# Turning k in 32x32 blocks on VectorE, and subtracting its low part on GpSimd, from the fifth pair of heads on

## The chip, the cores and the metric

One core of a Trainium2 chip. The metric is the device time of one execution in microseconds (us). The kernel before takes 958.05 us, the median of three runs (957.85 to 958.69).

## The reference

Three stages, all in fp32:

```
# decay attention: q, k, v are (4, 8, 576, 64), f is (4, 8, 576)
scores = q @ k.T / sqrt(64);  cum = cumsum(log(clip(f)))
scores = where(causal, -1e9, scores + cum[i] - cum[j])
attn   = softmax(scores);  x = attn @ v          # x then is (2304, 512)
# MLP 1:  h = max(x @ w_in, 0);  x = (h * h) @ w_out             (d_ff 2048)
# MLP 2:  x = (sigmoid(x @ w_gate) * (x @ w_val)) @ w_out2       (d_ff 1536)
```

The change is in the attention. 4 x 8 heads are 16 pairs of heads (p = 0 to 15).

## The kernel before, in words

fp32 products are computed as three products of reduced-precision parts: an operand x is split into a high part (a copy in the rounded type fp32r) and a low part (x minus the high part), and high-low, low-high and high-high are added up in PSUM. So each of q and k needs a high part (`qh`, `kh`) and a low part (`ql`, `kl`), both laid out with the 64 features of two heads on the 128 partitions and the 576 tokens along the free dimension.

**Loads.** `load(p, which)` (L275) brings q, k or v of a pair into `nat[...]`, tokens on partitions: two DMAs with runs of 256 bytes (L282) and one for the last 64 tokens (L286). q and k have two buffers, `nat["k"][p % 2]`. All DMAs are issued by SyncE (SP), which takes them in the order in which they are written and waits at each until its buffer is free.

**Turning.** `TQ` and `TK` turn q and k with five TensorE transposes each (L376, 128x128, with an identity matrix) into a PSUM tile; four PSUM tiles of [128, 1024] go round as a ring (`ps2`), each use waiting for the last reader of the one four uses earlier. Then ScalarE writes `qh` (L440) and `kh` (L467), and VectorE `ql` (L444) and `kl` (L471), all out of PSUM.

**The rest of a pair.** `S2`, `S3`, `S01` and `S4` (L416, L510) are score products of the query blocks; `R` (L390) on VectorE adds the causal mask and takes the row minimum (scores are negated); `X` (L398) is the exponential with row sums on ScalarE; `N0`, `N2`, `N3` (L519 a TENSOR_SCALAR, L520 a reciprocal) invert the row sums on VectorE; `M` (L528) multiplies the rows by them on GpSimd; `G1` to `G4` (L539, L545) are TensorE transposes of the result, in which G3 reads what M3a and M3b wrote and G4 what M4 wrote; `E1` to `E4` evacuate them (odd ones ScalarE L424, even ones VectorE L426); `PV` (L573) multiplies with v; `xhi` (L590, ScalarE) and `xlo` (L588, VectorE) split the output into parts. `EL` and `EH` (L452) copy the last 64 rows of ql and qh on GpSimd for S4.

**The order.** The order of all engines is written out by hand: the string `ORDER` lists the steps of one iteration, each with a lag (`TK-1` in iteration `it` works on pair it + 1, `PV+2` on pair it - 2), and each engine gets its instructions in that order. An iteration's PV is TensorE's first large piece in the listing below; PV of pair p belongs to iteration p + 2. `ahead` hangs pieces of weight preparation in front of a step: VectorE's four conversion operations of a weight block (L149, L150, L153, L156) stand one each ahead of `xlo` in iterations 5 to 8 and again 9 to 12, and GpSimd's subtractions (L630) ahead of `M0a` in iterations 10, 11, 14 and 15.

In the old order, ScalarE has X2a, xhi, qh, kh, X0a one after the other; VectorE has R0b, N3, xlo, ql, kl, R4; GpSimd has M0a, M1a, M1b, M2a, M2b, M0b, M3b, M3a, M4, EL, EH.

Of the kernel before, what the change touches and what calls it, by code (L numbers as in the profile page):

```python
# [9 lines left out]
F32 = mybir.dt.float32  # L10
# [3 lines left out]
AF = mybir.ActivationFunctionType  # L14
ALU = mybir.AluOpType
# [26 lines left out]
def kernel(  # L42
# [13 lines left out]
    nc = tc.nc  # L56
    B, H, S, D = q.shape
    NT, DM = out.shape
    BH = B * H
    NP = BH // 2  # L60
# [186 lines left out]
    def tiles(n, name, shape, dt=F32):  # L247
        return [ap_.tile(shape, dt, name=f"{name}{i}") for i in range(n)]

    nat = {nm_: tiles(3 if nm_ == "v" else 2, nm_ + "n", [128, NC, 2, D]) for nm_ in "qkv"}  # L250
    qk = [{nm_: ap_.tile([128, S], F32R, name=f"{nm_}{i}") for nm_ in ("qh", "ql", "kh", "kl", "cr")} for i in range(2)]
# [15 lines left out]
    cum_b = pts[0:BH, 6 * S:6 * S + 3 * HALF].bitcast(BF16)  # L267

    ring = [0]

    def ps2():
        ring[0] += 1
        return pair_t[(ring[0] - 1) % 4]

    def load(p, which):  # L275
        b, h0 = divmod(2 * p, H)
        for src, nm_ in ((q, "q"), (k, "k"), (v, "v")):
            if nm_ not in which:
                continue
            t = nat[nm_][p % len(nat[nm_])]  # L280
            for i in range(2):
                nc.sync.dma_start(  # L282
                    out=t[:, 0:NF, i, :],
                    in_=src[b, h0 + i, 0:NF * 128, :].rearrange("(c p) d -> p c d", p=128),
                )
            nc.sync.dma_start(  # L286
                out=t[0:REM, NF, :, :],
                in_=src[b, h0:h0 + 2, NF * 128:S, :].rearrange("h p d -> p h d"),
            )
# [28 lines left out]
    def setup():  # L318
# [8 lines left out]
        for nm_ in "qk":  # L327
            for t in nat[nm_]:
                nc.gpsimd.memset(t[64:128, NF, :, :], 0.0)
        load(0, "qk")  # L330
        nc.vector.tensor_reduce(out=nm_t[0][:, 0:1], in_=ident[:, 0:111:22], axis=mybir.AxisListType.X, op=ALU.add)
        nc.vector.tensor_scalar(one_l, one_l.bitcast(F32), nm_t[0][:, 0:1], None, op0=ALU.mult)
# [10 lines left out]
        for nm_ in ("eh", "el"):  # L343
            nc.gpsimd.memset(qk[0][nm_].bitcast(F32), 0.0)
        cum_v = cum_s.bitcast(F32).rearrange("p (t s) -> p t s", t=3)
        load(1, "q")
        cr_load(0, cum_v)
        load(1, "k")
        cr_load(1, cum_v)
        nc.gpsimd.memset(maskc, 0.0)  # L350
# [23 lines left out]
    def transpose_in(t, x):  # L374
        for c in range(NC):
            nc.tensor.transpose(x[:, 128 * c:128 * c + 128], t[:, c, :, :].rearrange("p h d -> p (h d)"), ident)  # L376
        return x[:, 0:S]
# [24 lines left out]
    live = {}  # L402
# [25 lines left out]

    def TQ(p):
        x = ps2()  # L430
        live["kt", p] = ps2()
        if p > 2:
            live["s4", p - 1] = ps2()
            s4_decay(p - 1)
        live["q", p] = transpose_in(nat["q"][p % 2], x)
        if p + 2 < NP and p != 1:
            load(p + 2, "q")
# [20 lines left out]
        ends(p, "el", "ql")  # L458

    def TK(p):  # L460
        live["k", p] = transpose_in(nat["k"][p % 2], live.pop(("kt", p)))
        if p + 2 < NP and p != 1:
            load(p + 2, "k")

    def kh(p):
        d = qk[p % 2]
        nc.scalar.activation(out=d["kh"], in_=live["k", p], func=AF.Copy)  # L467

    def kl(p):
        d = qk[p % 2]  # L470
        nc.vector.tensor_tensor(out=d["kl"], in0=live.pop(("k", p)), in1=d["kh"].bitcast(F32), op=ALU.subtract)  # L471

    def S01(p):
        s = live.pop(("s01", p))
# [20 lines left out]
    def s4_decay(p):  # L495
        s = live["s4", p]
        for g in range(2):
            a, b = decay(p, slice(0, 128), slice(64, 192), slice(g * HALF, (g + 1) * HALF))
            nc.tensor.matmul(s[:, 512 * g:512 * g + HALF], lhsT=a, rhs=b, start=True, stop=False)
# [81 lines left out]
    def x_part(p, low):  # L581
# [8 lines left out]
                nc.scalar.activation(out=x[:, 0, xs], in_=i, func=AF.Copy)  # L590

    STEP = {
        "CR": CR, "TQ": TQ, "qh": qh, "ql": ql, "EH": EH, "EL": EL, "TK": TK, "kh": kh, "kl": kl,
        "S01": S01, "S2": S2, "S3": S3, "S4": S4, "PV": PV,
        "xhi": lambda p: x_part(p, 0), "xlo": lambda p: x_part(p, 1),
        "N0": lambda p: N(p, 0, 4), "N2": lambda p: N(p, 4, 6),
# [6 lines left out]
    for g in range(1, 5):  # L603
        STEP[f"G{g}"] = lambda p, g=g: G(p, g)
        STEP[f"E{g}"] = lambda p, g=g: E(p, g)
    ORDER = """
        CR-1 R3a+1 X3a+1 S01+0 R2a+0 M0a+1 R2b+0 X2a+0 M1a+1 PV+2 N3f+1 xhi+2 M1b+1 R1b+0 R1a+0
        R0a+0 R0b+0 N3+1 TQ-1 TK-1 M2a+1 qh-1 kh-1 M2b+1 S4+0 M0b+1 xlo+2 X0a+0 ql-1 G1+1 X1a+0 kl-1
        X0b+0 M3b+1 M3a+1 E1+1 G2+1 G3+1 M4+1 X1b+0 R4+0 E3+1 G4+1 E2+1 N0+0 S3+0 X2b+0 EL-1 X4+0
        E4+1 S2-1 R3b+0 N2+0 X3b+0 EH-1  # L610
    """.split()
# [23 lines left out]
    for m in range(2):  # L635
        b = 4 + 4 * m
# [22 lines left out]
    for it in range(min(lags), NP + max(lags)):  # L659
# [6 lines left out]
        for nm_, lag in steps:  # L666
            p = it - lag
# [129 lines left out]
    late = []  # L797
# [438 lines left out]
    for n, (z, key, m) in enumerate(items):  # L1236
# [12 lines left out]
        elif m % 2:  # L1249
            at(*slot(z + 6), *[part_fn(w_sum, key, m // 2, x) for x in range(4)])  # L1250
            for x in range(4):
                p = 42 * (m // 2) + x - 1
# [244 lines left out]
    for i, (j, u) in enumerate(dsteps):  # L1497
# [43 lines left out]
        for c in range(2 if i == 0 else 0, 3):  # L1541
            o = down(i, c)
            if u == NU2 - 1:
                e = rs[c]
# [61 lines left out]
```

## Time and profile before

| | |
|---|---|
| median of three runs | 958.05 us |
| the profiled execution | 958.46 us, of which its span is 956.7 us |
| TensorE matmul busy | 949.4 us (99%) |
| VectorE / ScalarE / GpSimd busy | 734.9 / 560.8 / 329.1 us |
| attention stage | the first 180 us or so |
| granted TensorE clock | 1.0 of full speed |

All times in the listings are us from the start of the span; a row of a timeline is start, length, engine, line, operation, output <- input, shapes and count, and in brackets the idle time of the engine before it with the engine whose work ended that idle time. A row can hold several instructions of one line (x3).

### The profile page before, as it was taken

The numbers are of one execution on the slowest core, as the hardware profiler recorded it, in microseconds if no ns is written. First come the engines' busy times: TensorE is split into PE (matmuls) and PEld (weight loads), VectorE is DVE, ScalarE is ACT, GpSimd is POOL, SyncE is SP. The second block draws the span as 40 slices with busy tenths as digits, with TensorE's granted clock in tenths as the row PEclk, the third lists the DMA queues.
The fourth block names the chain that finished last, engine by engine and source line by source line (L and its number), as shares of the span: only waits on it lengthen the run. The fifth ranks groups of instructions, "written<-read, shape, count | busy, mean of one in ns | idle before, by whom it ended". The sixth has DMA issues, their size and how long they took to land.

```text
span 956.7 us, 18030 instructions
## 1 busy us (share of the span) xinstructions
PE 949.4 (99%) x6315; PEld 912.9 (95%) x6315; DVE 734.9 (77%) x1458; ACT 560.8 (59%) x1148; POOL 329.1 (34%) x427
## 2 busy tenths in 40 slices
PE   8999999999999999999999999999999999999998
PEld 7888888999999999999999999999999999889998
DVE  7889888376666676688879989767676777698895
ACT  7888888476565665566556556544445455354432
POOL 8777878112111120047023255634243341300000
PEclk9999999999999999999999999999999999999999
DMA  5633330287888889667776612334333345764441
GB/s 124 167 88 90 90 85 17 64 260 253 275 271 276 272 276 314 216 202 208 229 220 196 190 56 95 124 105 144 116 116 127 125 168 198 256 220 143 149 133 67
DMA packets 159618, 160.88 MB, mean 168 GB/s; under 512 B 66312, under 2 KB 136284, under 8 KB 159528
## 3 DMA queue, kind: packets, MB, share of 16 engines
q1 hardware_dynamic: 159528, 159.74, 54.2%
q8 instruction: 49, 0.80, 0.4%
q14 instruction: 41, 0.34, 0.1%
HBM read 102.93 MB, written 56.73 MB: 167 GB/s over the span
## 4 chain that ended last, share of the span: by engine, by line
PE 75%; DMA 10%; DVE 7%; ACT 4%; issue 2%; POOL 1%; SPq 0%; ACTq 0%; DVEq 0%
PE ps L1100 27%; PE ps L1046 13%; PE ps L1446 9%; PE ps L1322 5%; PE pa L573 5%; PE pa L416 4%; PE pa L539 4%; DMA g<-gt 3%; PE ps L220 3%; DMA gl<-g 2%; DVE gt L206 2%; DVE gg L742 2%; PE pa L376 1%; DMA wraw<-in_moe_w_in_dram 1%; DMA wraw<-in_moe_w_out_dram 1%
## 5 line engine op out<-in xcount | busy, mean ns | idle before, releaser
L220 PE MATMUL ps<-xT,hl 128*128 128x384 f32 x1104 | 191.5, 334 | 0.0
L220 PEld LDWEIGHTS ps<-xT,hl 128*128 128x128 f32 x1104 | 191.4, 188 | 0.0
L1046 PE MATMUL ps<-gg,ao 128*128 128x384 f32 x1008 | 175.8, 335 | 0.7 <-DVE gg L742 0.6
L1046 PEld LDWEIGHTS ps<-gg,ao 128*128 128x128 f32 x1008 | 174.5, 188 | 1.8 <-DVE gg L742 1.5
L528 POOL TENSOR_TENSOR pt<-pt,sm 128x128 f32<-128x128 f32 (+2 forms) x142 | 105.4, 769 | 33.2 <-DVE sm L520 27.2
L1100 PE MATMUL ps<-xT,r 128*128 128x384 f32 x576 | 107.5, 334 | 0.0
L742 DVE TENSOR_TENSOR gg<-gl,gg 128x768 fp32r<-128x768 f32 x78 | 81.9, 1055 | 28.4 <-ACT gg L741 28.1
L741 ACT ACTIVATE gg<-gl 128x768 fp32r<-128x768 f32 x78 | 66.0, 846 | 64.0 <-DMA gl<-g 30.1
L1100 PEld LDWEIGHTS ps<-xT,r 128*128 128x128 f32 x576 | 100.6, 188 | 0.1
L206 DVE TENSOR_TENSOR gt<-gt 128x384 f32<-128x384 f32 x96 | 53.6, 599 | 57.3 <-ACT gt L229 55.8
L398 ACT ACTIVATE pt<-pt,nm 128x384 f32<-128x384 f32 (+2 forms) x144 | 82.9, 582 | 3.7 <-DVE nm L390 3.2
L390 DVE CUSTOM_DVE_ANT_0 pt<-pa,maskc 128x384 f32<-128x384 f32 (+2 forms) x144 | 66.9, 514 | 3.5 <-PE pa L416 3.2
L132 ACT ACTIVATE wtmp<-wraw 128x512 f32<-128x512 f32 x66 | 43.9, 665 | 33.5 <-DMA wraw<-in_moe_w_in_dram 16.9
L177 POOL TENSOR_TENSOR hl<-wf,hl 128x512 fp32r<-128x512 f32 x14 | 18.1, 1295 | 129.2 <-ACT hl L173 129.2
L804 POOL TENSOR_TENSOR xT<-yt,xT 128x384 fp32r<-128x384 f32 x12 | 17.7, 1482 | 118.0 <-ACT xT L800 118.0
L1100 PE MATMUL ps<-xT,f 128*128 128x384 f32 x288 | 55.7, 334 | 0.0
L1100 PE MATMUL ps<-t,r 128*128 128x384 f32 x288 | 54.1, 334 | 0.0
L229 ACT ACTIVATE gt<-gt 128x384 f32<-128x384 f32 x96 | 50.5, 526 | 3.1
L1100 PEld LDWEIGHTS ps<-xT,f 128*128 128x128 f32 x288 | 50.4, 188 | 0.0
L1100 PEld LDWEIGHTS ps<-t,r 128*128 128x128 f32 x288 | 50.3, 188 | 0.1
L228 ACT ACTIVATE gt<-ps 128x384 f32<-128x384 f32 x92 | 43.9, 477 | 8.4 <-PE ps L220 7.0
L1424 ACT ACTIVATE xT<-x 128x896 fp32r<-128x896 f32 x27 | 25.7, 954 | 36.8 <-DVE x L1416 16.4
(257 smaller groups left out, 1959.1 us busy)
## 6 DMA issues: line engine op xcount, KB each, us to landing
gl<-g SPq DMA_DIRECT2D x90, 384.0 KB, 3.7
g<-gt SPq DMA_DIRECT2D x168, 192.0 KB, 4.8
wraw<-in_moe_w_out_dram SPq DMA_DIRECT2D x28, 512.0 KB, 4.7
x<-g SPq DMA_DIRECT2D x72, 128.0 KB, 2.7
wraw<-in_moe_w_in_dram SPq DMA_DIRECT2D x16, 512.0 KB, 4.5
wraw<-in_moe_w_val_dram SPq DMA_DIRECT2D x12, 512.0 KB, 4.4
g<-pb SPq DMA_DIRECT2D x29, 192.0 KB, 1.9
wraw<-in_moe_w_gate_dram SPq DMA_DIRECT2D x10, 512.0 KB, 4.0
```

What stands on the lines that cost most here:

```text
L206: nc.vector.tensor_tensor(out=t, in0=a, in1=b_, op=ALU.subtract)
L220: nc.tensor.matmul(h, lhsT=a, rhs=xT[c][:, b_, t0:t0 + BT], start=(c == 0 and i == 0), stop=(c == KD - 1 and i == 2))
L229: nc.scalar.activation(out=r, in_=r, func=AF.Square)
L390: nc.vector.tensor_tensor_reduce(out=o, in0=s, in1=mask, scale=1.0, scalar=3.0e38, op0=ALU.add, op1=ALU.min, accum_out=nm_t[p % 2][:, c:c ...
L398: nc.scalar.activation(out=x, in_=x, func=AF.Exp, bias=nm_t[p % 2][:, c:c + 1], scale=-1.0, accum_out=sm_t[p % 2][:, c:c + 1])
L528: nc.gpsimd.tensor_tensor(out=x, in0=x, in1=sm_t[p % 2][:, c:c + 1].to_broadcast([128, e - a]), op=ALU.mult)
L573: nc.tensor.matmul(o[64 * h:64 * h + 64, 512 * half + s - lo:512 * half + hi - lo], lhsT=vn[:, c, h, :], rhs=pts[:, h * PW + c * PS + s:h ...
L741: nc.scalar.activation(out=s[:, 0], in_=t, func=AF.Copy)
L742: nc.vector.tensor_tensor(out=s[:, 1], in0=t, in1=s.bitcast(F32)[:, 0], op=ALU.subtract)
L1046: nc.tensor.matmul(o, lhsT=ws[:, a, u, cs], rhs=s[:, b_, u, :], start=(k_ in (0, 2, 5) and w == u == x == 0), stop=(w == NW - 1 and u == 1 ...
L1100: nc.tensor.matmul(o, lhsT=w[p][:, a, ws], rhs=operand(n, jj, b_, c), start=(first and c == x == 0), stop=(c == 1 and x == 2), skip_group_ ...
L1446: nc.tensor.matmul(o, lhsT=YR[i % 4][:, a, FROM[n]], rhs=b_op(n, u, b_), start=(x == u == y == 0), stop=(u == NU2 - 1 and y == 2), skip_gr ...
```

## The change

From pair TP = 4 on k is not loaded with tokens on partitions but in four DMAs, one for each quarter of 32 partitions: partition 32r + i holds, for the 18 blocks of 32 tokens, the 32 features of quarter r of token 32b + i, in runs of 128 bytes. One VectorE instruction (`TKv`) then turns each 32x32 block in place, so that the features of two heads stand on the partitions, in SBUF. `TK` does nothing for these pairs and the PSUM tile that it used is not taken from the ring. `kh` (new step `khe`) reads SBUF on ScalarE, placed after X2a and ahead of xhi; `kl` (new step `kle`) is a GpSimd subtraction, placed after M0b and ahead of M3b; the load of the pair after next follows it. Pairs 0 to 3 are as before.

```diff
+    TP = 4
+
+    def k_flat(p):
+        return nat["k"][p % 2].rearrange("p c h d -> p (c h d)")[:, 0:S]
...
             t = nat[nm_][p % len(nat[nm_])]
+            if nm_ == "k" and p >= TP:
+                for r in range(4):
+                    h, e = divmod(r, 2)
+                    nc.sync.dma_start(
+                        out=k_flat(p)[32 * r:32 * r + 32, :].rearrange("p (b j) -> p b j", j=32),
+                        in_=src[b, h0 + h, :, 32 * e:32 * e + 32].rearrange("(b i) j -> i b j", i=32),
+                    )
+                continue
...
     def TQ(p):
         x = ps2()
-        live["kt", p] = ps2()
+        if p < TP:
+            live["kt", p] = ps2()
...
     def TK(p):
+        if p >= TP:
+            return
...
+    def TKv(p):
+        if p >= TP:
+            nc.vector.transpose(out=k_flat(p), in_=k_flat(p))
+            live["k", p] = k_flat(p)
+
+    def kh(p, late):
+        if late == (p < TP):
+            nc.scalar.activation(out=qk[p % 2]["kh"], in_=live["k", p], func=AF.Copy)
+
+    def kl(p, late):
+        if late == (p < TP):
+            d, eng = qk[p % 2], nc.vector if late else nc.gpsimd
+            eng.tensor_tensor(out=d["kl"], in0=live.pop(("k", p)), in1=d["kh"].bitcast(F32), op=ALU.subtract)
+            if not late and p + 2 < NP:
+                load(p + 2, "k")
...
-        CR-1 R3a+1 X3a+1 S01+0 R2a+0 M0a+1 R2b+0 X2a+0 M1a+1 PV+2 N3f+1 xhi+2 M1b+1 R1b+0 R1a+0
-        R0a+0 R0b+0 N3+1 TQ-1 TK-1 M2a+1 qh-1 kh-1 M2b+1 S4+0 M0b+1 xlo+2 X0a+0 ql-1 G1+1 X1a+0 kl-1
+        CR-1 R3a+1 X3a+1 S01+0 R2a+0 M0a+1 R2b+0 X2a+0 M1a+1 PV+2 khe-1 N3f+1 xhi+2 M1b+1 R1b+0 R1a+0
+        R0a+0 R0b+0 N3+1 TKv-2 TQ-1 TK-1 M2a+1 qh-1 kh-1 M2b+1 S4+0 M0b+1 kle-1 xlo+2 X0a+0 ql-1 G1+1 X1a+0 kl-1
```

## Rows read from the trace of the kernel before

**Rows 1.** Busy time by stretch (stretch: length, then each engine, clock, DMA).
```profile
core 0: us, PE busy (x) PEld busy (x) DVE busy (x) ACT busy (x) POOL busy (x), PEclk, DMA share, GB/s
60.00:70.00 10.00, 10.00 (x103) 8.55 (x102) 8.98 (x31) 8.67 (x25) 7.25 (x13) 1.00 0.41 92
```

**Rows 2.** Chain of waits: start, length, what; the attention stage.
```profile
66.51 2.85 PE pa L573 x28
...
69.72 1.09 PE pa L376 x10
...
76.80 2.85 PE pa L573 x28
```

**Rows 3.** Timeline of PE's weight loads, G4 of two iterations.
```profile
83.81 0.58 PEld L545 LDWEIGHTS pa<-ident,pt 128*128 128x128 f32 x5
...
165.62 0.53 PEld L545 LDWEIGHTS pa<-ident,pt 128*128 128x128 f32 x5 [0.25 <-POOL pt L528]
```

**Rows 4.** Timeline of ACT: xhi, and the first instruction behind X2a.
```profile
79.70 0.71 ACT L590 ACTIVATE xT<-pa 128x256 fp32r<-128x256 f32 x2 [1.27 <-PE pa L573]
...
88.61 0.67 ACT L132 ACTIVATE wtmp<-wraw 128x512 f32<-128x512 f32 x1
```

**Rows 5.** Timeline of DVE: conversions, N3's first op, xlo, ql, kl.
```profile
58.67 0.40 DVE L149 TENSOR_SCALAR wtmp<-wtmp 128x512 f32<-128x512 f32 x1
...
78.96 0.17 DVE L519 TENSOR_SCALAR sm<-sm 128x3 f32<-128x3 f32 x1
...
79.25 0.66 DVE L153 SCALAR_TENSOR_TENSOR wtmp<-wraw,wtmp 128x512 int32<-128x512 int32 x1
80.45 0.82 DVE L588 TENSOR_TENSOR xT<-pa,xT 128x256 fp32r<-128x256 f32 x2 [0.53 <-PE pa L376]
81.28 0.76 DVE L444 SCALAR_TENSOR_TENSOR ql<-pa,qh 128x576 fp32r<-128x576 f32 x1
81.95 0.75 DVE L471 TENSOR_TENSOR kl<-pa,kh 128x576 fp32r<-128x576 f32 x1
```

**Rows 6.** Timeline of POOL: M3b, M3a, M4 thrice, and M2a, M2b, M0b.
```profile
48.65 3.14 POOL L528 TENSOR_TENSOR pt<-pt,sm 128x512 f32<-128x512 f32 x3 [1.01 <-DVE sm L520]
...
79.50 3.41 POOL L528 TENSOR_TENSOR pt<-pt,sm 128x512 f32<-128x512 f32 x3 [1.01 <-DVE sm L520]
...
86.81 1.97 POOL L528 TENSOR_TENSOR pt<-pt,sm 128x384 f32<-128x384 f32 x3 [0.40 <-DVE sm L520]
...
162.42 3.14 POOL L528 TENSOR_TENSOR pt<-pt,sm 128x512 f32<-128x512 f32 x3 [1.30 <-PE pa L573]
```

**Rows 7.** Groups of POOL by shape: count | busy us, mean ns | idle.
```profile
L177 POOL TENSOR_TENSOR hl<-wf,hl 128x512 fp32r<-128x512 f32 x14 | 18.1, 1295 | 129.2 <-ACT hl L173 129.2
...
L630 POOL TENSOR_TENSOR hl<-wf,hl 128x128 fp32r<-128x128 f32 x8 | 3.5, 454 | 0.3
```

**Rows 8.** Groups of ACT that read SBUF, columns as before.
```profile
L173 ACT ACTIVATE hl<-wf 128x512 fp32r<-128x512 f32 x2 | 1.3, 632 | 0.0
...
L741 ACT ACTIVATE gg<-gl 128x768 fp32r<-128x768 f32 x78 | 66.0, 846 | 64.0 <-DMA gl<-g 30.1
```

**Rows 9.** Timelines of ACT and POOL: a subtraction that waits for ACT.
```profile
194.30 0.63 ACT L173 ACTIVATE hl<-wf 128x512 fp32r<-128x512 f32 x1 [0.60 <-DVE wf L156]
...
195.01 1.30 POOL L177 TENSOR_TENSOR hl<-wf,hl 128x512 fp32r<-128x512 f32 x1 [23.38 <-ACT hl L173]
```

**Rows 10.** Timelines of POOL and DVE: N0 of iteration 14 beside GpSimd.
```profile
155.99 0.87 POOL L630 TENSOR_TENSOR hl<-wf,hl 128x128 fp32r<-128x128 f32 x2
...
156.42 0.46 DVE L519 TENSOR_SCALAR sm<-sm 128x4 f32<-128x4 f32 x1
```

**Rows 11.** Timeline of SP: the load of k.
```profile
103.75 1.10 SPq L282 DMA_DIRECT2D kn<-in_k_dram  x2
104.96 0.61 SPq L286 DMA_DIRECT2D kn<-in_k_dram  x1
```

**Rows 12.** DMA issues, 100 to 140: count, KB each, us to landing.
```profile
kn<-in_k_dram SPq DMA_DIRECT2D x8, 128.0 KB, 2.4
```

More of the change, by code (lines that the diff above doesn't have):

```diff
@@ L463, in TK @@
             load(p + 2, "k")
[L465 to L471, printed above, removed]
+    def TKv(p):
[11 more added lines that the diff above has]
+                load(p + 2, "k")
     def S01(p):
@@ L592 @@
     STEP = {
-        "CR": CR, "TQ": TQ, "qh": qh, "ql": ql, "EH": EH, "EL": EL, "TK": TK, "kh": kh, "kl": kl,
+        "CR": CR, "TQ": TQ, "qh": qh, "ql": ql, "EH": EH, "EL": EL, "TK": TK, "TKv": TKv,
+        "kh": lambda p: kh(p, True), "khe": lambda p: kh(p, False),
+        "kl": lambda p: kl(p, True), "kle": lambda p: kl(p, False),
         "S01": S01, "S2": S2, "S3": S3, "S4": S4, "PV": PV,
```

## The prediction

> **What bounds the kernel now.** I read the stretches of 10 us first: in the attention stage TensorE (PE) is busy for 10.00 of 10 us, VectorE (DVE), ScalarE (ACT) and GpSimd (POOL) for 9.0, 8.7 and 7.3 [rows 1]. Then the chain of waits over that stage: it is PE and nothing else, one pair of heads after the other, with PV(p) starting at 66.51 and at 76.80, so 10.29 us a pair [rows 2]. In it the turning of q and k (TQ, TK: ten transposes, one piece) takes 1.09 us, k's five half of it, 0.545. A busy PE only says that nobody keeps it waiting, not by how much, so the next question is how late its operands come. The timelines of PE's weight loads, ACT, DVE and POOL answer that, and there the reader should look for idle times: ACT's before xhi (1.27 us), DVE's before xlo (0.53 here), POOL's before M3b (1.01) [rows 4 to 6]. The change puts one new piece of work into each of these three holes.
>
> **What the change takes from PE.** Pairs 4 to 15, in iterations 3 to 14, lose five transposes: 12 x 0.545 = 6.5 us if PE stays the bound, 9.745 us a pair.
>
> **DVE.** kl leaves: 0.75 us, starting 0.67 after ql [rows 5]. The turn in 32x32 blocks (TKv) comes, 128x576 from SBUF to SBUF. The trace shows none. The nearest row is kl itself, 0.75 for the same 576; the cheapest op of SBUF alone is L149 with 0.40 for 512, so 0.45 for 576 [rows 5]; twice kl, if a turn passes the data twice, is 1.5. I take 0.70, nearest to kl, and keep 0.45 and 1.5 as the ends. It stands in DVE's queue between N3 and xlo, where DVE idles anyway because xlo waits for xhi. In the eight iterations that also hold a weight-conversion op there, xlo slips by some 0.2 us. ql, behind it, now ends at 82.04 [rows 5], and what needs it first is G3: its eight transposes lie before G4's 83.81 [rows 3], at 0.11 each from 82.9. So 0.9 us of slip are free and the turn costs nothing; at 1.5 us the eight iterations would slip by 1.0 and lose 0.1 each, 0.8 in all. DVE's load, 9.0 a pair now, stays at 9.0 (9.8 at the upper end), below what follows.
>
> **ACT.** kh moves from behind qh to before xhi, reading SBUF: 0.632 for 512 and 0.846 for 768 [rows 8] give 0.685 for 576. The hole of 1.27 us hides it. But its start is fixed: behind X2a, where the next ACT instruction can start at 88.61 [rows 4].
>
> **POOL.** kl becomes a subtraction of two SBUF operands here (kle): 0.454 for 128 and 1.295 for 512 [rows 7], 2.19 ns an element, so 1.435 for 576; the multiplications M of the same engine come out cheaper (3.14 for 512+512+576 [rows 6]), about 1.15 for 576, which I keep as the lower end; the upper, 1.7, adds the 0.27 of the next paragraph but one. It stands behind M0b (group at 86.81, ends 88.78) and ahead of M3b, M3a, M4, and it waits for kh. So a wait is added at POOL's queue, and behind it are the M's that feed G3 and G4 on PE, then EL and EH, which only the next iteration's S4 reads.
>
> **The sum.** These holes are not free time, because what is behind kle in POOL's queue sets G4. The loop from one G4 to the next: G4's weights at 83.81, then S3, R3b, N2, R3a, X3a, X2a, up to the slot for kh at 88.61: 4.80 [rows 3, 4]. kh 0.685. ACT to POOL 0.08 (194.30 + 0.63 to 195.01 [rows 9]). kle 1.40 (1.435, less 0.04 by which POOL's neighbours overlap). M3b, M3a, M4: 3.14 [rows 6]. POOL to PE 0.06 (162.42 + 3.14 to 165.62 [rows 3, 6]). Together 10.16 us a pair. That is above the 9.745 of PE and only just below the 10.29 of now. So PE, which gets to G3 and G4 0.545 earlier, waits there for POOL. The last row of PE's weight loads has it already: in the iteration without q and k to turn, PE came 1.09 earlier and stood 0.25 before G4 for POOL [rows 3]. Gain 12 x 0.13 = 1.6 us. The sister loop through G3 and E3 lacks M4 and is shorter.
>
> Against it: in the pair at 79.50 the three M's took 3.41, not 3.14, with the conversion op of L153 (two SBUF operands on DVE, from 79.25) beside them [rows 5, 6]. Now M3b's delay is absorbed; behind kle it is on the loop. Four iterations have such an op: 4 x 0.27 = 1.1 us back. Net 0.5 us.
> The Trainium skill (SBUF — State Buffer, SBUF: two separate sides) calls this an exclusive lock of a port pair, taken by a VectorE op with two SBUF inputs or in a two-port mode, against a GpSimd op. The 0.27 agrees with a lock of which M3b's start-up hides a part (0.41 of the op was left). By that rule in full the four would cost 1.6, and the net be zero.
>
> **Queue and buffers.** SP issues v, q, k, cr in order; k's three DMAs become four, 2304 runs of 128 bytes for 1152 of 256. k's first issue (103.75) is past kle's end already, so the new wait on POOL holds up nobody; cr goes some 0.5 later and is read an iteration on. At 0.5 to 0.61 each [rows 11] the last issue ends near 106.1, lands at 108.5 with 2.4 us [rows 12], and TKv wants it 0.16 before M3b's start at 79.50, three periods on: 110.2. Between no more cost per byte and the same cost per run, landing is 2.4 to 4.8 us: from 1.7 early to 0.7 late, and ql has 0.9. Nothing. The PSUM ring loses one of eleven allocations a pair; G3 now waits for ql's buffer instead of kl's, which is earlier.
>
> All behind attention is PE at 99% and moves along. The profiled execution took 958.46 (span 956.7 and 1.76 around it); minus 0.5 is 957.96, and as the median of the runs lies 0.41 below it, 957.5.
>
> **Rivals.**
> 1. *PE stays the bound.* If kle costs like an M (1.15) and kh a little less, the loop is 9.85 or shorter and nearly all of the 6.5 us come: 951.5 to 954, price -5. For it: the idle times are of the size of the new work. Against: both prices of a two-operand POOL subtraction lie on one line.
> 2. *POOL's subtraction holds up VectorE (slower).* Where POOL ran a two-operand op from 155.99 to 156.86, the tiny TENSOR_SCALAR of N0 (0.17 elsewhere) took 0.46 and ended with it [rows 10]. N3's TENSOR_SCALAR starts at 78.96 [rows 5], kle by my sum at 88.61 + 0.765 - 10.29 = 79.08. If kle is first (from 0.12 us earlier on), N3 ends with kle, and from the end of that op to M3b's start the rows have 0.37 (79.13 to 79.50 [rows 5, 6]): with the overlap of 0.04 lost, M's 0.41 later. The loop is then 10.57, 0.28 above now, x 12 = 3.4; with the 1.1 of above, 4.5 on 958.05: 962.5. The same comes if the turn takes that port pair. For it: 0.12 is little. Against: N3 hangs on the same R3a as kh, so the order does not drift.
> By the Trainium skill (same page, Who interferes with whom) only two-port or two-input VectorE ops meet GpSimd there; a block turn is neither by what it says, and no row here shows one.
> 3. *k lands late.* Beyond 0.9 us of lateness TKv pushes ql and G3; it is late from 4.1 us to landing on, so at 5.5 it costs 0.5 a pair, 6 in all: 963.5. For it: runs half as long. Against: SP's queue idles in between.
>
> **How the numbers follow.** Likeliest, the loop through POOL takes PE's place: 0.50, 955.5 to 959.5 (the loop uncertain by 0.15, x 12). Rival 1: 0.22. Rival 2: 0.22. Rival 3: 0.06. What a measurement of this kernel can tell from no change is about 0.2%, 1.9 us: below 956.1 lie rival 1 and a third of the likeliest, 0.38; above 960.0 rivals 2 and 3 but for a little, 0.26; between, 0.36. Range 952 to 963, leaving out the lower end of rival 1 (0.05) and the upper of rivals 2 and 3 (0.13).
>
> **What would show it.** In the profile after: pair period near 10.16; idle of PE's weight loads at G3 or G4, released by POOL's M line, some 0.4 us a pair; POOL without its hole of 1.01 before M3b, kle of 1.43 starting 0.08 behind kh; TKv near 0.7 with DVE's hole before xlo gone. Wrong if kle is near 1.15 or PE shows no idle time (rival 1), if N3's TENSOR_SCALAR is stretched to over 1 us or kle to over 1.6 (rival 2), or if TKv waits for a DMA (rival 3).

## The result, and the profile after

The changed kernel takes 964.76 us (median of 6 runs, 962.81 to 967.72), the kernel before 958.17 beside it (6 runs, 957.85 to 959.99): ratio 1.0067, interval [1.0048, 1.0087]. It is slower by 6.6 us. The prediction, 957.5 in a range of 952 to 963, was wrong.

The profiled execution of after took 964.47 us (span 962.6), 6.0 more than that of before. Two starts in the chain of waits split it: those of the last PV, where the attention stage is nearly over. First before, then after (start, length, what).

```profile
177.42 2.86 PE pa L573 x28
```
```profile
180.59 2.86 PE pa L596 x28
```

3.2 us were lost up to here; from here to the end of the span it is 779.3 before and 782.0 after, 2.7 more. So two things went wrong, in two places.

**In the attention.** The stretch of 10 us of after that answers to [rows 1], same columns:

```profile
60.00:70.00 10.00, 9.90 (x100) 8.08 (x98) 9.17 (x32) 8.76 (x24) 8.89 (x14) 1.00 0.46 91
```

POOL went from 7.25 to 8.89, and PE and its weight loads (PEld) have gaps where PE had none. The chain of waits, all PE in [rows 2], now goes round through four engines (60 to 82):

```profile
59.91 0.58 ACT kh L487
60.49 0.07 issue
60.56 1.42 POOL kl L492
61.98 2.19 POOL pt L551 x2
64.17 0.04 issue
64.21 1.09 PE pa L562 x8
65.31 0.01 issue
65.32 0.76 PE pa L568 x5
66.08 1.05 PE pa L428 x7
67.13 0.02 issue
67.15 0.69 DVE pt L402
...
67.85 0.11 DVE sm L542
...
69.41 0.78 ACT pt L410 x3
70.19 0.58 ACT kh L487
```

That is the predicted loop but for one step: kh, the handoff of 0.07, kle, two M's, G3 and G4 (L562, L568), S3, R and N2 on VectorE (L402, L542), X on ScalarE, and kh again, 10.28 us later. The prediction went through all three M's straight to G4, and here two M's and G3 lead there; both ways arrive together (PE is through with G3 at 65.30, M4 ends at 65.27 by the timeline below). The weight loads of G3 and G4, for [rows 3], each stand waiting for GpSimd:

```profile
64.21 0.86 PEld L562 LDWEIGHTS pa<-ident,pt 128*128 128x128 f32 x8 [0.32 <-POOL pt L551]
65.32 0.53 PEld L568 LDWEIGHTS pa<-ident,pt 128*128 128x128 f32 x5 [0.25 <-POOL pt L551]
```

The three moved pieces, all twelve of each (instruction, count, shortest/median/longest ns, first and last start):

```profile
L482 DVE STREAM_TRANSPOSE kn<-kn x12: 778/778/780, 31.1 to 144.7; 128x576 f32<-128x576 f32 x12
L487 ACT ACTIVATE kh<-kn x12: 665/667/669, 39.6 to 154.1; 128x576 fp32r<-128x576 f32 x12
L492 POOL TENSOR_TENSOR kl<-kn,kh x12: 1412/1416/1422, 40.4 to 154.8; 128x576 fp32r<-128x576 f32 x12
```

Timelines of VectorE and then GpSimd, for [rows 5, 6], in a pair with a TENSOR_SCALAR conversion (L149) and in one with a two-operand one (L156):

```profile
60.44 0.16 DVE L542 TENSOR_SCALAR sm<-sm 128x3 f32<-128x3 f32 x1
60.64 0.18 DVE L543 RECIPROCAL sm<-sm 128x3 f32<-128x3 f32 x1
60.85 0.78 DVE L482 STREAM_TRANSPOSE kn<-kn 128x576 f32<-128x576 f32 x1
61.55 0.71 DVE L149 TENSOR_SCALAR wtmp<-wtmp 128x512 f32<-128x512 f32 x1
62.18 0.81 DVE L611 TENSOR_TENSOR xT<-pa,xT 128x256 fp32r<-128x256 f32 x2
...
92.66 0.97 DVE L156 SCALAR_TENSOR_TENSOR wf<-wraw,wtmp 128x512 int32<-128x512 int32 x1
```
```profile
60.56 1.42 POOL L492 TENSOR_TENSOR kl<-kn,kh 128x576 fp32r<-128x576 f32 x1 [0.65 <-ACT kh L487]
61.94 3.33 POOL L551 TENSOR_TENSOR pt<-pt,sm 128x512 f32<-128x512 f32 x3
...
91.67 1.42 POOL L492 TENSOR_TENSOR kl<-kn,kh 128x576 fp32r<-128x576 f32 x1 [0.65 <-ACT kh L487]
93.04 3.59 POOL L551 TENSOR_TENSOR pt<-pt,sm 128x512 f32<-128x512 f32 x3
```

The conversion starts while kle runs, ends 0.28 and 0.54 us after kle's end, and the M's behind kle take 3.33 and 3.59 instead of 3.14. The holes before xlo and M3b are gone. N3's TENSOR_SCALAR starts 0.12 ahead of kle and is not stretched.

The period from PV to PV shows what this makes of the loop (iterations 2 to 14, worked out from the weight loads of PV):

```
iteration   2     3     4     5     6     7     8     9     10    11    12    13    14
before    10.28 to 10.34 in all of them
after     12.74 10.06 10.11 10.28 10.28 10.55 10.55 10.28 10.56 10.81 10.57 10.11 10.36
extra work  -     -     -   TS    TS    2op   2op   TS    TS,W  2op,W 2op    -     W
```

TS is a TENSOR_SCALAR conversion on VectorE, 2op one with two SBUF operands, W GpSimd's own weight subtraction. A pair without any takes 10.06 to 10.11.

W costs its pair 0.27, and not in GpSimd's queue: there kle still waits 0.42 us for kh. W stands ahead of M0a and makes the next M's later, so that VectorE's TENSOR_SCALAR of N2, which is on the loop, now starts while one of them runs (GpSimd works on M's without a pause from 108.88 to 112.36). In the chain of waits it takes 0.39, 0.39 and 0.38 in the three pairs with W, and 0.10 to 0.12 in those without, as at 67.85 above. The chain and GpSimd's timeline in iteration 10:

```profile
109.51 0.39 DVE sm L542
```
```profile
112.78 1.42 POOL L492 TENSOR_TENSOR kl<-kn,kh 128x576 fp32r<-128x576 f32 x1 [0.42 <-ACT kh L487]
```

Iteration 2, with 2.44 us of the 3.2, is another matter: it holds the first block turn. Timelines of SP, VectorE and PE there:

```profile
26.66 2.16 SPq L288 DMA_DIRECT2D kn<-in_k_dram  x4
27.73 0.18 DVE L543 RECIPROCAL sm<-sm 128x3 f32<-128x3 f32 x1
31.07 0.78 DVE L482 STREAM_TRANSPOSE kn<-kn 128x576 f32<-128x576 f32 x1 [3.16 <-DMA vn<-in_v_dram]
32.70 2.39 PE L562 MATMUL pa<-ident,pt 128*128 128x128 f32 x20 [2.24 <-DVE xT L611]
```

The load of this k is issued from 26.66 to 28.82, and VectorE was ready to turn it at 27.91. (The row names the load of v, issued right behind it; the instruction reads only k, and the same wait in e2 below is put down to the load of k.) The later ones have their place: SP's row for the load at 64.69, and the turn at 71.13 that it feeds (not shown), are 6.4 us apart, and that turn does not wait.

```profile
64.69 2.17 SPq L288 DMA_DIRECT2D kn<-in_k_dram  x4
```

**Behind the attention.** In the down stage of the first MLP, TensorE multiplies `gg`, which ScalarE and VectorE make of `gl`, loaded from DRAM. Waits there, before and after (engine and line <- what ended the wait: us in total, times, longest; PEld from the end of the attention on, ACT from 376 to 550):

```profile
PEld ps L1046 <- DVE gg L742: 1.5, 3, 0.9
...
ACT gg L741 <- DMA gl<-g: 30.1, 25, 2.9
```
```profile
PEld ps L1071 <- DVE gg L767: 4.8, 9, 1.0
...
ACT gg L766 <- DMA gl<-g: 37.4, 29, 3.9
```

PE's waits for gg grew by 3.3 us; in the rest of the span behind the attention PE is as dense as before. No line of this stage was changed.

A load of gl needs one of a few buffers, and SP waits until VectorE, done with its part of gg, has given one back (108 us of such waits in this stage before, 111 after). So load, ScalarE, VectorE and the next load make a ring, and the chain of waits of after runs through it; a piece of it:

```profile
438.47 3.38 DMA gl<-g
...
441.95 0.86 ACT gg L766
442.83 1.53 DVE gg L767
444.38 3.66 DMA gl<-g
```

From 376 to 550 the loads of gl are 11.1% of the chain before and 22.7% after, PE's products 68.3% and 45.5%. This shows where the time is lost, not what brings the ring onto the chain more often.

### The profile page after: what moved, and what is told of

It reads as the page before. It is cut to its first block, busy times and chain, and to the rows that moved or that the text cites. A ratio compares the mean times of both kernels' runs of the same rounds, so it can differ in the third digit from the quotient of the medians.

```text
span 962.6 us, 17921 instructions
## 1 busy us (share of the span) xinstructions
PE 948.7 (99%) x6255; PEld 904.8 (94%) x6255; DVE 741.0 (77%) x1458; ACT 564.2 (59%) x1148; POOL 346.2 (36%) x439
## 4 chain that ended last, share of the span: by engine, by line
PE 80%; DVE 5%; DMA 5%; POOL 3%; ACT 3%; issue 1%; SPq 1%; ACTq 0%; DVEq 0%
PE ps L1125 27%; PE ps L220 20%; PE ps L1471 9%; PE ps L1071 9%; PE ps L1347 5%; DMA gl<-g 4%; PE pa L562 3%; PE pa L428 2%; POOL pt L551 2%; DVE gg L767 2%; PE pa L596 2%; POOL kl L492 1%; DVE pt L402 1%; ACT pt L410 1%; PE pa L568 1%
## 5 line engine op out<-in xcount | busy, mean ns | idle before, releaser
L1071 PE MATMUL ps<-gg,ao 128*128 128x384 f32 x1008 | 177.4, 335 | 2.2 <-DVE gg L767 2.0
L767 DVE TENSOR_TENSOR gg<-gl,gg 128x768 fp32r<-128x768 f32 x78 | 85.7, 1107 | 29.2 <-ACT gg L766 28.7
L402 DVE CUSTOM_DVE_ANT_0 pt<-pa,maskc 128x384 f32<-128x384 f32 (+2 forms) x144 | 66.9, 514 | 4.3 <-PE pa L428 4.3
L153 DVE SCALAR_TENSOR_TENSOR wtmp<-wraw,wtmp 128x512 int32<-128x512 int32 x66 | 47.0, 712 | 1.6
```

The costliest lines, as they stand in the source:

```text
L402: nc.vector.tensor_tensor_reduce(out=o, in0=s, in1=mask, scale=1.0, scalar=3.0e38, op0=ALU.add, op1=ALU.min, accum_out=nm_t[p % 2][:, c:c ...
L767: nc.vector.tensor_tensor(out=s[:, 1], in0=t, in1=s.bitcast(F32)[:, 0], op=ALU.subtract)
L1071: nc.tensor.matmul(o, lhsT=ws[:, a, u, cs], rhs=s[:, b_, u, :], start=(k_ in (0, 2, 5) and w == u == x == 0), stop=(w == NW - 1 and u == 1 ...
```

## The experiments

All ratios are to the kernel before, run beside each kernel (medians of 958.16 to 958.73). "Attention" is the start of the last PV, and "behind" the rest of the span, in the one profiled execution of each kernel: 177.4 and 779.3 for before, 180.6 and 782.0 for after. The kernels of the experiments are called e1 to e18.

**Which place?** Both kernels with the MLP stages left out (the attention ends by storing the high part of its output):

```diff
+    for c in range(KD):
+        nc.sync.dma_start(out=ov[:, c, :], in_=xT[c].bitcast(F32)[:, 0, :])
     att.close()
-    psp = ctx.enter_context(tc.tile_pool(name="psp", bufs=1, space=PSUM, reuse_waits="tile"))
...
```

> The kernel before without the two MLP stages (it stops behind the attention and stores the high part of its result). Alone it says little: some 190 to 200 us; it is what the next two are set against.

> The changed kernel cut in the same way. The profiles give the attention 3.2 us more than before (2.4 at the first turn, 1.0 in the loop, 0.3 back at the end), and the rest of the 6.6 arises behind it. If so, 3.2 above the cut kernel before, within 0.5. Rival: the attention varies from run to run and holds all of it in the median: 6 to 7 above.

Before (e5) 202.36 us (202.31 to 202.44), after (e6) 204.73 (204.16 to 205.62). So the attention costs 2.4 of the 6.6 us, and 4.2 arise behind it. The 3.2 expected were those of one execution: in the profile of e6 iteration 2 took 11.27 us, 1.0 too much instead of 2.4, so the first stall varies from one execution to another.

**Is it the loop?** kle goes behind M4, off the loop:

```diff
-  ... S4+0 M0b+1 kle-1 xlo+2 ...  M4+1 X1b+0 ...
+  ... S4+0 M0b+1 xlo+2 ...  M4+1 kle-1 X1b+0 ...
```

> The changed kernel with GpSimd's subtraction moved behind M4 (ahead of EL), all else alike. If the loop G4, S3, R3b, R3a, X3a, X2a, kh, kl, M3b, M3a, M4, G4 sets the period, kl is off it now: the period falls to TensorE's own 9.75 (9.9 where GpSimd has the weight subtractions too), 12 x 0.5 = 6 us less than the changed kernel: 958.5, or 956 without the late term; TensorE no longer waits for M at G3 and G4, and M3b waits for N3's reciprocal again. Rival: GpSimd and VectorE hold each other up wherever the subtraction stands, or TensorE gains nothing by fewer transposes: period 10.1 to 10.5, 963 to 965.

This kernel, e2, takes 960.16 us (958.04 to 963.14), ratio 1.0018 [1.0004, 1.0031]. Its chain of waits from 80 to 99 is PE alone again; one pair of it:

```profile
81.31 0.80 PE pa L533 x6
82.11 2.37 PE pa L562 x20
84.48 0.55 PE pa L568 x5
85.03 2.46 PE pa L428 x30
87.49 2.86 PE pa L596 x28
90.34 0.35 PE pa L522 x2
90.69 0.55 PE pa L388 x5
```

GpSimd's timeline there, kle behind the M's:

```profile
80.28 3.60 POOL L551 TENSOR_TENSOR pt<-pt,sm 128x512 f32<-128x512 f32 x3 [0.38 <-DVE sm L543]
83.84 1.41 POOL L492 TENSOR_TENSOR kl<-kn,kh 128x576 fp32r<-128x576 f32 x1
```

The period is 9.74 to 10.0 in ten of the twelve pairs, six of them at the 9.75 that PE alone gives, although the M's beside the conversion are as long as in after (3.60): off the loop that no longer sets the pair. What is left above 9.75 (up to 10.42 in iteration 11) stands in pairs with a conversion or a weight subtraction; in four places PE waits there for xlo, 1.3 us in all, which comes behind the turn and the conversion on VectorE. Attention 175.6. So it was the loop that held the pairs at 10.1 to 10.8. But behind the attention it has 783.3, 4.0 more than before, and the first turn still stalls (iteration 2: 12.82). The same edit with the MLP stages left out:

> The same cut for the kernel with kl behind M4. By its profile the attention ends 1.8 us earlier than before: 1.8 below the cut kernel before, within 0.5, though the whole kernel was 1.6 slower. Rival: the attention is no faster in the median: 0 to 1.6 above.

This one, e7, takes 200.05 us (199.48 to 200.94), 2.3 below the cut before. So what e2 wins in the attention it gives back behind it.

**Is the first stall SP's late start?** The block turn from the seventh pair on, by when SP is less far behind:

```diff
-    TP = 4
+    TP = 6
```

> The changed kernel with the turn on VectorE from pair 6 on instead of pair 4. What the trace of the changed kernel suggests: its 6.6 us are three terms: 2.4 where the first turn (pair 4, in iteration 2) waited 3.2 us for its load of k, which SyncE issued late at the start; 0.7 in the pairs after it (loop through kh, kl, M, G4: 10.1 to 10.8 us a pair against 10.29); 2.7 later, in the first down stage of the MLP, where TensorE waited 6.8 us for split operands against 2.1 before. By this the first term goes, the pairs from iteration 5 on cost 1.1 as they did: 962.0 if the late term stays, 959.3 if that is tied to the stall. Rival: the load in runs of 128 bytes is too slow wherever the first one stands, then the stall moves to iteration 4 and the time stays at 964 to 965.

This kernel, e1, takes 961.08 us (959.88 to 962.68), ratio 1.0024 [1.0015, 1.0034]. No stall; VectorE goes straight on to its first turn, whose load is issued from 42.93 on, 5.8 us before it is wanted:

```profile
48.55 0.18 DVE L543 RECIPROCAL sm<-sm 128x3 f32<-128x3 f32 x1
48.76 0.78 DVE L482 STREAM_TRANSPOSE kn<-kn 128x576 f32<-128x576 f32 x1
```

Attention 178.7, 1.3 later than before: the loop's cost alone. Behind: 778.8, 0.5 less than before. So in this execution the term behind the attention is gone as well, for which the loop and the stall give no reason. It was the fastest of the nine, though; the median is 1.2 longer, and where that lies is not shown.

**Both edits**, kle behind M4 and TP = 6:

> Both remedies: kl behind M4, and the turn on VectorE from pair 6 on. By the periods measured one at a time (iterations 5 to 14 at 9.94 on average against 10.30 in the kernel before, no stall at the first turn) the attention is 3.4 us shorter than before; 955.1 if the MLP stage takes what it took before, 956.3 if it takes 1.2 more as with the turn from pair 6 alone. Rival: the first turn stalls because TensorE comes earlier, or the MLP stage takes back all of it: 958 to 959.

This kernel, e8, takes 955.35 us (954.52 to 956.40), ratio 0.9967 [0.9954, 0.9979]: faster than both kernels. Attention 173.8, behind 779.9.

Two more ways to spare the first stall with kle behind M4: TP = 5 (e12), and TP = 4 with the first turn alone moved to the head of the next iteration (e9).

```diff
-    def TKv(p):
-        if p >= TP:
+    def TKv(p, first=False):
+        if p >= TP and first == (p == TP):
...
+        "TKw": lambda p: TKv(p, True),
...
-        CR-1 R3a+1 X3a+1 S01+0 ...
+        CR-1 TKw-1 R3a+1 X3a+1 S01+0 ...
```

> kl behind M4, the turn on VectorE from pair 5 on: eleven pairs. Its first turn is in iteration 3. Its load is issued by iteration 2's TK; if SyncE has caught up by then: attention 3.9 us shorter than before, 954.6 to 955.5. If the first turn stalls by 1 to 2 us as with pair 4: 956 to 957, and 959 or more if the late term comes with it.

> kl behind M4, the turn on VectorE from pair 4 on, but the first turn (pair 4) one iteration later, at the head of iteration 3, when its load has long landed. By the first term of the account the stall of 1 to 2.5 us in iteration 2 goes, for 0.8 of VectorE once: the attention 4 us shorter than before. 954.2 if the late term of 4 us (whole kernel against attention alone) belongs to the stall, 958 if it belongs to having twelve pairs turned. Rival: the stall moves to the next pair, 956 to 960.

No stall like that in either: the first turn of e12 waits 0.40 us (its load is issued from 34.16, 4.0 before it is wanted), that of e9 not at all. TP = 5: 957.86 us (956.73 to 958.98), ratio 0.9991 [0.9981, 1.0000], attention 173.4, behind 781.7. First turn moved: 958.53 (957.48 to 960.97), ratio 0.9999 [0.9988, 1.0009], attention 174.5 (two pairs at 10.78 and 10.34; in the first of them the turn waits 0.5 for k), behind 781.5. Both attentions are about as good as that of e8; behind them both lose 2.2 to 2.4 us to before. Against their expectations, e12 missed all that was named, and e9 came out where twelve turned pairs bring the late term without the stall.

The block turn behind ql instead of ahead of xlo, on e8 (e15):

```diff
-  ... N3+1 TKv-2 TQ-1 ... ql-1 G1+1 ...
+  ... N3+1 TQ-1 ... ql-1 TKv-2 G1+1 ...
```

> kl behind M4 and the turn from pair 6 on, with the turn moved on VectorE from ahead of xlo to behind ql. k has 1.9 us more to land, and xlo and ql no longer wait behind the turn: TensorE's waits for xlo at G3 (1.6 us in the profile) go, 954. Rival: VectorE has its idle time ahead of xlo and none behind ql, so R4, E2 and E4 come 0.7 later and lengthen the period: 957 to 959.

955.27 us (954.86 to 957.89), ratio 0.9972 [0.9963, 0.9981]: no different from e8. PE's weight loads no longer wait for xlo (1.6 us between 60 and 160 in e8), but most pairs are 9.92 to 10.15: nothing is won.

**What makes TensorE wait behind the attention?** Four single suspects, each put into a kernel of which the rest is unchanged. Runs of 128 bytes (e3): the kernel before, with k loaded in halves of 32 features from the fifth pair on.

```diff
+  for e in range(2 if nm_ == "k" and p >= 4 else 1):
+      ds = slice(32 * e, 32 * e + 32) if nm_ == "k" and p >= 4 else slice(0, D)
...
```

> The kernel before, with k from pair 4 on loaded in runs of 128 bytes (two DMAs of 32 features for each head in place of one of 64), turned and used as before. The transfer alone. If the 128-byte runs cost nothing by themselves: 958.2, within 0.6, and TensorE's waits in the MLP's down stage at 2 us. Rival: the doubled number of pieces slows the load, or the late term of the MLP stage comes from it: 960.5 to 962.

959.40 us (958.11 to 962.47), ratio 1.0012 [1.0002, 1.0021]: 0.9 us by the medians, 2.0 at the upper end of the interval, so a part of the 4.2 at most. (Its profiled execution was its longest one, 962.47: attention 179.5, with two pairs over 11 near the start, and behind 781.2.)

More DMAs (e10): the kernel before, with cr_load twice from the fifth pair on.

```diff
+        if p > 3:
+            cr_load(p, cum_d)
```

> The kernel before, with the small load of the decay rows issued twice from pair 4 on: 12 further DMAs of 6.8 KB, as many as the change adds for k. If the late term came from the number of DMAs on SyncE's queue: 961 to 962, TensorE waiting 5 us or more in the MLP's first down stage. If not: 958.2, waits of 2 to 3 us.

958.30 us (957.53 to 960.39), ratio 0.9995 [0.9985, 1.0004]: nothing. These DMAs are small ones, though. A delay (e4): the kernel before, with k of pair 4 turned six times on TensorE.

```diff
+        for _ in range(6 if p == 4 else 1):
...
```

> The kernel before, in which TensorE turns k of pair 4 six times in place of once (25 further transposes of 0.109 us, the result the same): a delay of 2.7 us in the attention and nothing else. If a delay only passes on to the end: 960.9, waits in the MLP's down stage at 2 us. Rival: the MLP stage's late term comes with any shift of the attention's end against what runs beside it: 963 to 964, waits there at 5 to 7 us.

962.05 us (961.58 to 962.41), ratio 1.0032 [1.0019, 1.0044]. In its profile the pair took 2.7 us more and the stage behind 0.9 more: a delay is passed on, and mostly no more than that. A stall of VectorE as at the first turn (e11): e8 with xlo of pair 0 written four times.

```diff
-            if low:
+            for _ in range((4 if p == 0 else 1) if low else 0):
...
```

> kl behind M4 and the turn from pair 6 on (955.35), with VectorE held up by about 2.3 us in iteration 2, where the changed kernel's first turn waits (xlo of pair 0 is written four times in place of once). If a stall there passes on and nothing else: 957.6. If the late term of 4 us comes with a stall of VectorE at this place: 960 to 961.5.

959.58 us (957.07 to 961.07), ratio 1.0007 [0.9996, 1.0017], 4.2 above e8. The stall came out at 4.3 us instead of the 2.3 meant, and it is all in the attention (178.2); behind is 779.3, as in e8 or less.

The fifth suspect is the number of TensorE's instructions: turning fewer pairs on TensorE shifts all that follow. `busy(16)` in the setup issues 16 matmuls that nobody reads; taking five away (below) or adding five (`busy(21)`) shifts by as many as one pair's turning.

```diff
-        busy(16)
+        busy(11)
```

On e8 with 11 (e13), on e9 with 21 (e14):

> kl behind M4 and the turn from pair 6 on (955.4), with 5 of the 16 warming matmuls of the setup left out, so that TensorE's program is as many instructions shorter than before's as with twelve turned pairs. The late term of 2 to 4 us was there in all four profiles with 11 or 12 turned pairs and in none of the three with 10. If it follows the place of TensorE's later instructions in its program: 957.5 to 959. If it follows the number of pairs turned, or is chance: 955.4.

> kl behind M4, twelve pairs, the first turn an iteration later (958.5), with 5 further warming matmuls in the setup, so that TensorE's program is as long as with ten turned pairs. By the place in the program: the late term of 2.3 goes, 955.5 to 956.5. By the number of pairs, or chance: 958.5.

e8 with five less: 956.98 us (955.77 to 958.10), ratio 0.9987 [0.9977, 0.9996], 1.6 worse with the same attention (173.8); behind 781.3. e9 with five more: 957.05 (955.42 to 960.87), ratio 0.9988 [0.9976, 0.9999]. Each set against the kernel before beside it, that is 0.9 better than e9, with intervals that overlap; its attention is 0.5 earlier and behind is 781.3, hardly less. Both came out between what the place in the program and the number of turned pairs had given, so they settle nothing. So, on before (e16, e17) and on after (e18):

> The kernel before with 11 warming matmuls in the setup in place of 16; nothing else. If the MLP's down stage feels where TensorE's instructions stand in the program: 959.5 to 961.5. If not: 958.2.

> The kernel before with 21 warming matmuls in place of 16. Same question, the other way: 957 to 961 if the place counts, with no sign known; 958.2 if not (the matmuls stand beside the first loads; at worst 0.5 more).

> The changed kernel with 21 warming matmuls in place of 16, so that TensorE's program is 50 matmuls shorter than before's, as with ten turned pairs, and not 60. If its late term of 4 us goes with the place: 961 to 963. If it goes with the change itself: 964.8.

Before with five less: 959.80 us (958.18 to 963.80), ratio 1.0017 [1.0005, 1.0028], attention the same, behind 780.4. Before with five more: 958.64 (958.09 to 960.80), ratio 1.0007 [0.9997, 1.0016], behind 779.1. After with five more: 964.57 (963.50 to 966.73), ratio 1.0068 [1.0053, 1.0083], behind 783.0, and PE's wait for gg is as long as ever:

```profile
PEld ps L1071 <- DVE gg L767: 5.9, 12, 1.1
```

Five instructions less on TensorE went with about 1.5 us more in two kernels (e16 with an interval of 0.5 to 2.7), five more with no clear change in before and in after. That does not explain the 4.2 us of after.

## Why the prediction was wrong, by its steps

**What bounds the kernel now**: right. **What the change takes from PE**: right; half of e2's twelve pairs run at the 9.745 worked out.

**DVE**: TKv 0.78 for 0.70, near the row that it was taken from. "The turn costs nothing" holds in the loop; in e2, with nothing else in the way, xlo begins to hold G up a little (1.3 us in 4 places).

**ACT and POOL**: kh 0.667 for 0.685, kle 1.416 for 1.435, the handoff 0.07 for 0.08. The line through two prices of the same form held, for kh between them and for kle a little beyond, and the nearest rows were the right ones. Rival 1 fell with that.

**The sum**: the mechanism is right (G3, behind two M's, binds as closely as G4), and the clean pair too, 10.06 to 10.11 for 10.16. The loop's gain, "12 x 0.13 = 1.6", would have been about 2.4 (12 pairs at 10.09, against the mean of 10.29). The step that failed is the term against it, "Four iterations have such an op: 4 x 0.27 = 1.1 us back". What came back is 3.4, by the table of periods:

- Four pairs with a two-operand conversion lose about 0.46 each, not 0.27. The row that the 0.27 is from [rows 5, 6] had the op start ahead of the M's, so that part of it was over before them; behind kle the op starts in kle's time, is held up until kle ends, and comes out on top of M3b.
- Four pairs with a TENSOR_SCALAR conversion lose 0.19 each. The prediction gave them no price. L149 itself takes 0.71 for 0.40.
- Three pairs, in which GpSimd also has a weight subtraction, lose 0.27 each, by which VectorE's TENSOR_SCALAR of N2 is held up beside GpSimd. That is the stretching of [rows 10]; the prediction looked for it at N3 only, and N2 is on the loop as well.

4 x 0.46 + 4 x 0.19 + 3 x 0.27 = 3.4, so the pairs lost 1.0 instead of gaining 0.5. The Trainium skill (SBUF — State Buffer, SBUF: two separate sides) has the shared port pair held as an exclusive lock for a whole instruction, by GpSimd or by a VectorE op that has two SBUF inputs or runs in a two-port mode. The trace agrees with it better than the row that was preferred to it: L149 and L156 end 0.28 and 0.54 after kle, as if only then begun, with the M's longer by 0.19 and 0.45. The block turn, 778 ns with kle beside it in eleven pairs and without it in the first, is outside it.

**Queue and buffers**: "Nothing" is the second failed step. The lateness was worked out at one place, 103.75 to 110.2, where SP has idle time, and there it is right (6.4 us from issue to turn, no wait). The first turned pair stands where SP is still issuing back to back (the rows from 20 to 34 have no gap over 0.1): first issue at 26.66, wanted at 27.91, turned at 31.07. From first issue to turn these are 4.4 us, and e12's waiting first turn has the same 4.4 (34.16 to 38.59): what was short was not the transfer but the head start. k from tokens had a whole iteration more there, since TK works on the next pair and TKv on the one after it. This cost 2.44 us in the profile and 1.0 in the cut kernel's; e1 and e9 take it away, e12 all but 0.4. It is rival 3, for one pair instead of twelve.

**"All behind attention is PE at 99% and moves along"**: the third, and the largest: 4.2 us by the cut kernels, 2.7 in the one profiled execution. PE's 99% hid that the down stage gets gg just in time (1.5 us of waits already before). Shown is that the time is lost there: in the 17 profiles of whole kernels, behind is 778.8 to 779.3 us where PE waits 1.4 to 1.9 us for VectorE's gg, 782.0 at 4.8 (after), 783.0 at 5.9 (e18) and 783.3 at 6.3 (e2), and the others lie between. ACT's waits for gl do not tell as much (36.0 in e15, which loses nothing). Not shown is why. Small DMAs (e10), a delay (e4) and a VectorE stall (e11) do not bring it, the runs of 128 bytes alone (e3) at most a part; the place of TensorE's instructions moves it by some 1.5 us on other kernels and not on after (e13, e16 against e18). Behind the attention, kernels with ten pairs turned have -0.5 to +0.6 over before (but e13 +2.0), with eleven or twelve +2.0 to +4.0. These are single profiles. Whether that is the count of turned pairs or how the loads come to lie is open.

**Rival 2**: N3's TENSOR_SCALAR comes 0.12 ahead of kle, as worked out, and takes 0.16: refuted at that place. The same holding up came at N2 in the three pairs with W, 0.8 us in all. The kernel came out slower as this rival had it, but for the most part for other reasons.

The version that beats both is e8 (or e15), 955.3 us, 0.3% under before: kle off the loop, and the first block turn where its load is issued early enough.

## What to carry to other kernels

Before work is moved into the idle time of an engine, close the loop that goes through it: an idle time ahead of a wait is the slack of that loop, and once it is spent, other pieces come onto the path: what holds that engine up, and what it holds up on the other engines of the loop. A load that is needed earlier must be looked at where the queue is fullest, most of all at the start, and not in the steady state. Where a later stage waits for its operands even a little, don't assume that it moves along unchanged: cut the kernel there and time both parts.

## What was not expected of the hardware

- A VectorE block turn of 128x576 fp32, SBUF to SBUF, takes 0.778 us, all twelve within 2 ns, eleven of them with GpSimd's two-operand subtraction beside it and the first without.
- Five TensorE instructions less at the very start, which change nothing in the attention, went with 1.4 (before) and 1.6 us (e8) more, which the profiles show behind it. Why is open.
